# Chunk attention: half-row sums shared between GpSimd and VectorE, and an order planned with longer VectorE durations

## The chip, the cores and the metric

The kernel runs on one core of a Trainium2 chip. The metric is device time in microseconds (us), lower is better. A profiled execution gives the trace from which every row below comes; its times are those of that one execution.

## The reference, cut to what matters

Three layers run one after the other on 8 sequences of 576 tokens. Only the first one and the routing of the second are touched.

```python
# 1. attention inside chunks of 64 tokens, 8 heads of 64
scores = scale * np.matmul(q_c, k_c.transpose(0, 1, 2, 4, 3))
scores = scores - np.max(scores, axis=-1, keepdims=True)
attn = np.exp(scores)
attn = attn / (np.sum(attn, axis=-1, keepdims=True) + 1e-09)
out = np.matmul(attn, v_c)
# 2. one of 8 experts per token; a token takes a fresh choice or the choice of the token before it
h = np.maximum(x[b, s] @ w1[e], 0.0)
out[b, s] = p[e] * (h @ w2[e])
# 3. four causal attention experts, the two best mixed per token
```

## The kernel before, in words

**Stages.** `chunk_attention` (line 166) works through 36 tiles of 128 tokens. The expert layer follows, then the causal mix. In the trace the first stage with all routing lasts until about 234 us, the experts until 660 us, the mix to the end.

**A tile.** q and k are loaded in pairs of tiles, turned by TensorE (L277) and copied out by ScalarE (L292, L295). TensorE makes the scores (L315). VectorE takes the row maximum (L326, 512 columns on 128 partitions, 64 per head) and subtracts it (L330). ScalarE takes the exponential (L334). Then VectorE sums each row of exponentials (L335), adds 1e-9 (L336) and takes the reciprocal (L337). Meanwhile TensorE turns the exponentials (L261 `at`), they are copied out (L344), multiplied by v (L354), and VectorE scales the product by the reciprocal (L363, tile `xs`). GpSimd issues the store of `xs` to the scratch tensor `x_d` (L368). TensorE turns `xs` too (L261 `xs`), and L390 and L405 make the gate logits, which VectorE collects (L408, tile `L`).

**Routing.** After every 9 tiles `route_group` (line 482) runs a chain of small steps that goes back and forth between VectorE and TensorE: from L504 through the turn L523, the scans L534, the turns L541 and L554, the choice L564 to L573, the counts L580 and L584, to the bit split L601 to L605 and the table `lo` (L619). After the third of four groups `route_early` (line 658) sums slot numbers for the first expert by 27 matmuls (L670, the early slot sum) and VectorE turns them into row indices (L652 to L656, `gfirst`). With these GpSimd fetches rows of `x_d` (L703). Two blocks of 256 tokens of the first expert are computed while the last tiles and the last routing group still run: `early_pair` (line 675) turns the fetched rows (L715), multiplies by w1 (96 matmuls of 256 columns a block, written L1620 to L1622, "up" here) and, for the first block, by w2 (48 matmuls of 512 columns, "down"). `route_all` (line 786) takes all four groups: VectorE builds the one-hot slot table (L817) and its products (L823; half on GpSimd), TensorE sums it by 36 matmuls (L832, the full slot sum), VectorE makes `gidx` (L655), GpSimd fetches the next block's rows (L839), and the first instruction of the expert stage on TensorE turns them (L954).

**Order.** None of this is issued in the order of the code. Every step is put into a `Plan` with an engine, a cost in us, a due key and the steps and buffers it waits for; `emit` picks, step by step, the earliest start by these costs, and the order that comes out is fixed for each engine. Engines then run in that order and wait by semaphores. So a cost in the code moves instructions but does not change how long one takes.

Of the kernel before, what the change touches and what calls it, by code (L numbers as in the profile page):

```python
# [14 lines left out]
OP = mybir.AluOpType  # L15
AX = mybir.AxisListType
# [97 lines left out]
class Model:  # L114
# [51 lines left out]
    def chunk_attention(self):  # L166
# [5 lines left out]
        with ExitStack() as ctx:  # L172
# [11 lines left out]
            R = {name: Ring(n) for name, n in (("q", 2), ("k", 2), ("tq", 2), ("one", 4),  # L184
                                               ("qT", 2), ("st", 5), ("at", 4), ("aT", 2), ("xs", 3), ("xT", 2), ("lp", 2))}

# [117 lines left out]
            def token_tile(t):  # L304
# [29 lines left out]
                x = plan.add("ACT", act(512), lambda: A.activation(box["at"], box["at"], AF.Exp, scale=0.125), t, [d2])  # L334
                d3 = plan.add("DVE", dve(512), lambda: V.tensor_reduce(box["st"][:, 1], box["at"], axis=AX.X, op=OP.add), t + 0.5, [x])  # L335
                d4 = plan.add("DVE", 0.08, lambda: V.tensor_scalar(box["st"][:, 1], box["st"][:, 1], 1e-9, None, op0=OP.add), t + 1.5, [d3])  # L336
                d5 = plan.add("DVE", 0.12, lambda: V.reciprocal(box["st"][:, 2], box["st"][:, 1]), t + 1.5, [d4])  # L337

# [7 lines left out]
                tp.users.append(y)  # L346
                sat.users += [ft, d3]
                px = R["px"].slot()
# [133 lines left out]
    def route_group(self, g):  # L482
# [18 lines left out]
        def bank():  # L501
            return self.psum(RING, [128, 512])
        small, mid = 0.08, 0.145
        step("DVE", mid, lambda: V.tensor_reduce(r["mx"], Lg, axis=AX.X, op=OP.max))  # L504
# [13 lines left out]
        box = {}  # L518
# [13 lines left out]
        def scans():  # L532
            box["kp"], box["sv"] = T([GT, 128], "kp"), T([GT, 128], "sv")
            V.tensor_tensor_scan(box["kp"], box["pr"][:, 1], r["zeros"], 1.0, op0=OP.mult, op1=OP.add)  # L534
            V.tensor_tensor_scan(box["sv"], box["pr"][:, 1], box["rise"], 0.0, op0=OP.mult, op1=OP.add)
        q.users.append(step("DVE", 0.4, scans))
        q = R[RING].slot()
# [24 lines left out]
        def chosen():  # L562
            box["ef"] = T([GT, 128], "rise")
            V.scalar_tensor_tensor(box["ef"], box["kp"], box["cin"], box["sv"], op0=OP.mult, op1=OP.add)  # L564
        step("DVE", 0.26, chosen)
        q = R[RING].slot()
# [31 lines left out]
        def bits():  # L598
# [6 lines left out]
            V.tensor_copy(r["hi"][:, ts], si[:, 2])  # L605
        ranked = step("DVE", 0.6, bits)
        self.placed = getattr(self, "placed", [])
        if g < self.NG - 1:
            K = self.K

            def early():
                x = r["erows"][:, ts, 0]
                V.tensor_tensor(x, r["hi"][:, ts, None].to_broadcast([128, GT, K]),
                                r["slotn"][:, None, :K].to_broadcast([128, GT, K]), op=OP.is_equal)
                V.tensor_tensor(x, x, oh[:, 0, :, None].to_broadcast([128, GT, K]), op=OP.mult)
                V.tensor_tensor(r["erows"][:, ts, 1], x, r["tnum"][:, ts, None].to_broadcast([128, GT, K]), op=OP.mult)
                V.tensor_scalar(x, x, r["part"], None, op0=OP.mult)
            self.placed.append(step("DVE", 0.45, early))
        low = step("DVE", 1.27, lambda: V.tensor_tensor(r["lo"][:, ts], r["lane"][:, None, :].to_broadcast([128, GT, 128]),  # L619
                                                        box["sf"][:, :, None].to_broadcast([128, GT, 128]), op=OP.is_equal))  # L620
# [37 lines left out]
    def route_early(self):  # L658
# [8 lines left out]
        def gather():  # L667
            x = box["pi"] = self.psum(self.RING, [128, 512])[:, :2 * K]
            for t in range(n):
                nc.tensor.matmul(x, r["lo"][:, t], r["erows"][:, t].rearrange("p a s -> p (a s)"), start=t == 0, stop=t == n - 1)  # L670
        step("PE", 0.064 * n, gather, takes=[q])
        self.early_at = step("DVE", 0.5, lambda: self.places(box["pi"].rearrange("p (a s) -> p a s", a=2), K, self.gfirst, self.sfirst))
        q.users.append(self.early_at)
# [1018 lines left out]
```

## Time and profile before

| | |
|---|---|
| median of 3 runs | 1083.32 us (1082.28 to 1086.37) |
| the profiled execution | 1081.1 us |
| its span | 1079.3 us |
| TensorE busy | 1027.4 us, 95% |
| VectorE busy | 689.1 us, 64% |
| ScalarE busy | 596.9 us, 55% |
| GpSimd busy | 337.1 us, 31% |

TensorE's matmuls overlap each other, so its busy time is time in which at least one of them runs. Its idle time, and its granted clock, are what the other engines and the order cost. VectorE's share is an average: it is far higher in the first stage than later.

### The profile page before, as it was taken

The page shows a single profiled execution, that of the slowest core. Times are in us where ns is not written, and L with a number is a line of the kernel's source. Part 1 is how long each engine was busy: PE and PEld are TensorE (multiplying, and loading weights), DVE is VectorE, ACT ScalarE, POOL GpSimd, SP SyncE. Part 2 cuts the span into 40 slices and gives each one's busy share as a digit, 9 for nine tenths or more (in the row PEclk, how much of TensorE's full clock was granted, in tenths as well). Part 3 has the DMA queues.
Part 4 walks back from the last instruction along what each step waited for, and adds up shares of the span by engine and source line. Part 5 has one row for each costly group of instructions (what it writes and reads, how often), then busy time and mean ns, then how long its engine had stood idle before and what let it go on. Part 6 is the DMA issues. An engine that isn't in the chain of part 4 may idle for free. (4 is left out here: it accounts for less than half of the span.)

```text
span 1079.3 us, 23454 instructions
## 1 busy us (share of the span) xinstructions
PE 1027.4 (95%) x7767; PEld 917.6 (85%) x7767; DVE 689.1 (64%) x1770; ACT 596.9 (55%) x1379; POOL 337.1 (31%) x586
## 2 busy tenths in 40 slices
PE   7999897999999998999999999999999999999996
PEld 5877776899899887998898996988999999999985
DVE  6678888564552245435623421597888888898884
ACT  5988986223441135315512310577777777777774
POOL 3111354232242232322422312143334243343431
PEclk9999998999999999999999999999999999999998
DMA  9999982145543154334622311434252432525231
GB/s 222 232 253 242 267 247 87 59 144 177 181 140 128 42 163 134 131 128 141 216 98 99 116 49 54 125 84 100 66 137 70 127 86 93 122 67 127 65 84 50
DMA packets 136476, 138.98 MB, mean 129 GB/s; under 512 B 54724, under 2 KB 108024, under 8 KB 134264
## 3 DMA queue, kind: packets, MB, share of 16 engines
q1 hardware_dynamic: 116584, 99.66, 34.3%
q0 software_dynamic: 12592, 35.18, 9.8%
q10 hardware_dynamic: 7136, 2.11, 0.8%
q8 instruction: 84, 1.38, 0.5%
q14 instruction: 80, 0.66, 0.2%
HBM read 89.70 MB, written 29.64 MB: 111 GB/s over the span
## 5 line engine op out<-in xcount | busy, mean ns | idle before, releaser
L1620 PE MATMUL ph<-xh,w 128*128 128x256 f32 x512 | 142.4, 278 | 4.4 <-ACTq L1062 2.6
L1622 PE MATMUL ph<-xh,w 128*128 128x256 f32 x512 | 142.3, 278 | 0.3 <-DVE w L877 0.3
L1621 PE MATMUL ph<-xl,w 128*128 128x256 f32 x512 | 142.0, 277 | 0.0
L970 ACT ACTIVATE hh<-ph 128x512 fp32r<-128x512 f32 x64 | 37.9, 598 | 182.7 <-PE ph L1622 182.6
L1042 POOL DMA_INDIRECT y_d<-ys,sidx x39 | 39.5, 1012 | 284.2 <-DVE ys L1037 213.4
L1453 POOL TENSOR_SCALAR a<-a,st,g_out 128x128 f32<-128x128 f32 (+3 forms) x128 | 79.5, 622 | 85.4 <-DVE st L1448 58.6
L1032 PE MATMUL py<-w,hh 128*128 128x512 f32 x280 | 104.5, 398 | 0.3 <-issue 0.3
L971 DVE SCALAR_TENSOR_TENSOR hl<-ph,hh 128x512 fp32r<-128x512 f32 x64 | 43.4, 688 | 93.8 <-ACT hh L970 65.3
L1620 PEld LDWEIGHTS ph<-xh,w 128*128 128x128 f32 x512 | 96.1, 188 | 6.5 <-ACTq L1062 3.8
L1622 PEld LDWEIGHTS ph<-xh,w 128*128 128x128 f32 x512 | 96.5, 189 | 0.5 <-DVE w L877 0.5
L1621 PEld LDWEIGHTS ph<-xl,w 128*128 128x128 f32 x512 | 96.3, 188 | 0.5
L1037 DVE TENSOR_SCALAR ys<-py,pg 128x512 f32<-128x512 f32 x37 | 27.7, 749 | 104.5 <-PE py L1034 82.3
L1437 ACT ACTIVATE a<-sc,st 128x256 f32<-128x256 f32 (+4 forms) x160 | 83.0, 521 | 20.4 <-DVE st L1429 14.9
L1032 PE MATMUL py<-w,hl 128*128 128x512 f32 x232 | 90.9, 392 | 0.0
L1429 DVE TENSOR_REDUCE st<-sc 128x1 f32<-128x256 f32 (+4 forms) x160 | 75.8, 482 | 4.4
L877 DVE TENSOR_TENSOR w<-raw,w 128x512 fp32r<-128x512 f32 (+1 forms) x84 | 67.1, 865 | 16.6 <-ACT w L876 12.2
L1252 ACT ACTIVATE at<-tp 128x128 fp32r<-128x128 f32 (+2 forms) x144 | 65.1, 455 | 22.4 <-PE tp L1470 20.4
L1253 DVE TENSOR_TENSOR at<-tp,at 128x128 fp32r<-128x128 f32 (+2 forms) x144 | 72.3, 505 | 7.5 <-ACT at L1252 6.1
L1470 PE MATMUL tp<-ident,a 128*128 128x128 f32 (+1 forms) x400 | 69.6, 276 | 7.2 <-DVE at L1253 3.5
L1034 PE MATMUL py<-w,hh 128*128 128x512 f32 x280 | 69.8, 391 | 0.0
L1418 PE MATMUL sc<-kd,qs 128*128 128x128 f32 (+3 forms) x256 | 62.8, 338 | 4.2 <-ACT a L1437 3.4
L876 ACT ACTIVATE w<-raw 128x512 fp32r<-128x512 f32 (+1 forms) x84 | 57.3, 761 | 16.9 <-DMA wst<-in_moe_wq_dram 6.0
(335 smaller groups left out, 2881.6 us busy)
## 6 DMA issues: line engine op xcount, KB each, us to landing
raw<-in_moe_w_dram SPq DMA_DIRECT2D x32, 1024.0 KB, 6.6
kd<-kb SPq DMA_DIRECT2D x64, 160.0 KB, 3.0
vb<-in_v_dram SPq DMA_DIRECT2D x144, 64.0 KB, 4.4
x_d<-xs POOLq DMA_DIRECT2D x36, 256.0 KB, 4.0
yt<-y_d SPq DMA_DIRECT2D x32, 256.0 KB, 2.7
kd<-kb SPq DMA_DIRECT2D x64, 128.0 KB, 2.4
out_dram<-zs SPq DMA_DIRECT2D x32, 256.0 KB, 2.0
q<-in_q_dram SPq DMA_DIRECT2D x11, 512.0 KB, 5.5
```

The lines of the kernel that those rows point to most:

```text
L877: (engine or self.nc.vector).tensor_tensor(lo, src, as_f32(hi), op=OP.subtract)
L1032: nc.tensor.matmul(py[m], h[:, j, ms], W2[0][:, j], start=h is hh and j == 0, stop=False)
L1034: nc.tensor.matmul(py[m], hh[:, j, ms], W2[1][:, j], start=False, stop=j == JF - 1)
L1252: h = plan.add("ACT", act(n), lambda: A.activation(hi, src(), AF.Copy), key, dep)
L1253: l = plan.add("DVE", dve(n), lambda: V.tensor_tensor(lo, src(), as_f32(hi), op=OP.subtract), key, [h])
L1429: V.tensor_reduce(st[:, i:i + 1], box["sc"][i][:, :k1 - k0], axis=AX.X, op=OP.max, negate=True)
L1437: A.activation(a[:, k0:k1], box["sc"][i][:, :k1 - k0], AF.Exp, bias=st[:, 0:1], accum_out=st[:, 3 + i:4 + i])
L1453: (P if ext <= PX else V).tensor_scalar(a[:, :ext], a[:, :ext], st[:, 6:7], gate, op0=OP.mult, op1=OP.mult)
L1470: nc.tensor.transpose(ta[:c1 - c0, kc - k0], box["a"][:, c0:c1], self.ident)
L1620: self.nc.tensor.matmul(out, ah, bh, start=first and i == 0, stop=False)
L1621: self.nc.tensor.matmul(out, ah, bl, start=False, stop=False)
L1622: self.nc.tensor.matmul(out, al, bh, start=False, stop=last and i == n - 1)
```

## The change

The sum of each row of 64 exponentials is split. GpSimd adds the two halves of each row (two inputs of 256 columns, new tile `half`, one buffer), VectorE sums the 32 that are left (256 columns instead of 512), GpSimd adds the 1e-9, and VectorE takes the reciprocal. Apart from this only costs in the plan change, nearly all of them upward, and the `lp` ring has one buffer instead of two. In the changed kernel the lines after L335 stand 7 lower: the half sum is L341, 1e-9 is L343, the reciprocal L344, `xs` L370, the last gate turn L412, the turn of the routing L530, the row turn L722, the table `lo` L626, the full slot sum L839, the expert stage's first turn L961.

```diff
-               d3 = plan.add("DVE", dve(512), lambda: V.tensor_reduce(box["st"][:, 1], box["at"], axis=AX.X, op=OP.add), t + 0.5, [x])
-               d4 = plan.add("DVE", 0.08, lambda: V.tensor_scalar(box["st"][:, 1], box["st"][:, 1], 1e-9, None, op0=OP.add), t + 1.5, [d3])
-               d5 = plan.add("DVE", 0.12, lambda: V.reciprocal(box["st"][:, 2], box["st"][:, 1]), t + 1.5, [d4])
+               hslot = R["half"].slot()
+
+               def halve():
+                   box["half"] = sb("half", [128, H, C // 2])
+                   P.tensor_tensor(box["half"], box["at"][:, :, :C // 2], box["at"][:, :, C // 2:], op=OP.add)
+               d2 = plan.add("POOL", 0.55, halve, t + 0.5, [x], [hslot])
+               d3 = plan.add("DVE", dve(256), lambda: V.tensor_reduce(box["st"][:, 1], box["half"], axis=AX.X, op=OP.add), t + 0.5, [d2])
+               hslot.users.append(d3)
+               d4 = plan.add("POOL", 0.22, lambda: P.tensor_scalar(box["st"][:, 1], box["st"][:, 1], 1e-9, None, op0=OP.add), t + 1.5, [d3])
+               d5 = plan.add("DVE", 0.2, lambda: V.reciprocal(box["st"][:, 2], box["st"][:, 1]), t + 1.5, [d4])
...
-       small, mid = 0.08, 0.145
+       small, mid = 0.14, 0.17
...
-       q.users.append(step("DVE", 0.4, scans))
+       q.users.append(step("DVE", 0.75, scans))
...
-       ranked = step("DVE", 0.6, bits)
+       ranked = step("DVE", 0.85, bits)
...
-           self.placed.append(step("DVE", 0.45, early))
+           self.placed.append(step("DVE", 1.2, early))
...
-       step("PE", 0.064 * n, gather, takes=[q])
+       step("PE", 0.03 * n, gather, takes=[q])
```

What the new costs move is seen in the orders. The first place is VectorE (DVE) behind the second routing group, at the copy of its probabilities (`kp`) and after. `st` holds a tile's maxima, sums and reciprocals. Before:

```order
L326 TENSOR_REDUCE st<-one 128x8
L336 TENSOR_SCALAR st<-st 128x8
L326 TENSOR_REDUCE st<-one 128x8
L330 TENSOR_TENSOR at<-one,st 128x512
L363 TENSOR_TENSOR xs<-one,st 128x512
L337 RECIPROCAL st<-st 128x8
L330 TENSOR_TENSOR at<-one,st 128x512
L335 TENSOR_REDUCE st<-at 128x8
L363 TENSOR_TENSOR xs<-one,st 128x512
L344 COPY aT<-one 128x512
```

The same place in the changed kernel:

```order
L344 RECIPROCAL st<-st 128x8
L651 COPY kp<-one 9x128
L370 TENSOR_TENSOR xs<-one,st 128x512
L341 TENSOR_REDUCE st<-half 128x8
L326 TENSOR_REDUCE st<-one 128x8
L330 TENSOR_TENSOR at<-one,st 128x512
L344 RECIPROCAL st<-st 128x8
L370 TENSOR_TENSOR xs<-one,st 128x512
L326 TENSOR_REDUCE st<-one 128x8
L330 TENSOR_TENSOR at<-one,st 128x512
```

The sums read `half` instead of `at`, and the 1e-9 step is gone from VectorE.

The second place is TensorE (PE) between the last gate turn (`lp`) and the first turn of the last routing group (`keep`). `tq<-q,w` is an "up" matmul of the first early block, `tq<-w,raw` a "down" matmul. Before, 36 up matmuls stand between the two, the first and the last of them here:

```order
L405 MATMUL one<-ident,lp 128x128 x2
L1620 MATMUL tq<-q,w_0_83 128x256
...
L1622 MATMUL tq<-q,w_1_84 128x256
L523 MATMUL one<-ident,keep 9x128
L524 MATMUL one<-ident,w 9x128
```

In the changed kernel:

```order
L412 MATMUL one<-ident,lp 128x128 x2
L1627 MATMUL tq<-q,w_0_83 128x256
...
L1629 MATMUL tq<-q,w_1_84 128x256
L722 MATMUL one<-ident,raw_81 128x128 x8
L1627 MATMUL tq<-w_0_85,raw_3006 128x512
...
L530 MATMUL one<-ident,keep 9x128
L531 MATMUL one<-ident,w 9x128
```

Of the 96 up matmuls of the first block, 84 stand ahead of the last gate turn and 12 behind it (48 and 48 before), and 8 turns and 18 down matmuls have come ahead of `keep`.

The third place is TensorE at the full slot sum (`one<-raw,lo`), up to the first turn of the expert stage (`pxt`). Before, 48 up matmuls of the second early block stand between them:

```order
L832 MATMUL one<-raw_81,lo 128x108
L1620 MATMUL tq<-q,w_0_83 128x256
L1621 MATMUL tq<-k,w_0_83 128x256
...
L1622 MATMUL tq<-q,w_1_84 128x256
L954 MATMUL pxt<-ident,raw_81 128x128 x8
```

In the changed kernel:

```order
L1628 MATMUL tq<-k,w_0_83 128x256
L1629 MATMUL tq<-q,w_1_84 128x256
L839 LDWEIGHTS lo
...
L839 MATMUL one<-raw_81,lo 128x108
L961 MATMUL pxt<-ident,raw_81 128x128 x8
```

All 96 up matmuls of the second block stand ahead of the slot sum, and the expert stage's turns follow it directly.

## Rows read from the trace of the kernel before

**Rows 1.** Windows: busy us and instructions of each engine, TensorE's clock, DMA share, GB/s.

```profile
20.00:160.00 140.00, 131.13 (x1562) 107.28 (x1560) 113.14 (x294) 124.35 (x220) 34.89 (x52) 1.00 1.00 249
125.00:145.00 20.00, 16.26 (x191) 13.21 (x189) 19.86 (x52) 16.30 (x28) 7.75 (x8) 1.00 0.89 223
234.00:450.00 216.00, 211.76 (x1356) 190.87 (x1357) 94.58 (x130) 73.40 (x119) 63.10 (x62) 1.00 0.45 147
```

**Rows 2.** Timeline of TensorE: start us, us, instruction, idle before and its releaser.

```profile
90.56 1.09 PE L277 MATMUL tq<-ident,k 128*128 128x128 f32 x8 [1.87 <-ACT kb L295]
...
127.55 1.09 PE L277 MATMUL tq<-ident,q 128*128 128x128 f32 x8 [1.38 <-ACT qT L292]
...
143.87 0.66 PE L261 MATMUL one<-ident,xs 128*128 128x128 f32 x4 [1.09 <-DVE xs L363]
```

**Rows 3.** Groups by form: busy us, mean ns of one, idle before.

```profile
L335 DVE TENSOR_REDUCE st<-at 128x8 f32<-128x512 f32 x36 | 24.3, 678 | 8.9 <-ACT at L334 8.8
L336 DVE TENSOR_SCALAR st<-st 128x8 f32<-128x8 f32 x36 | 8.0, 224 | 0.2
L1429 DVE TENSOR_REDUCE st<-sc 128x1 f32<-128x256 f32 x48 | 20.2, 421 | 1.1
L900 POOL TENSOR_TENSOR w<-raw,w 128x512 fp32r<-128x512 f32 x8 | 10.2, 1281 | 10.1 <-ACT w L899 10.0
L1653 POOL TENSOR_TENSOR g_eq<-g_eq,lower 128x80 f32<-128x80 f32 x4 | 1.4, 358 | 0.6 <-DVE g_eq L1639 0.4
L1446 POOL TENSOR_SCALAR st<-st 128x1 f32<-128x1 f32 x144 | 31.3, 217 | 104.6 <-ACT a L1437 97.8 <-DVE sc L1427 1.1
```

**Rows 4.** Timeline of GpSimd and of VectorE at two of GpSimd's subtractions.

```profile
129.31 2.36 POOL L900 TENSOR_TENSOR w<-raw,w 128x1024 fp32r<-128x1024 f32 x1 [1.45 <-ACT w L899]
...
140.24 2.37 POOL L900 TENSOR_TENSOR w<-raw,w 128x1024 fp32r<-128x1024 f32 x1 [0.80 <-ACT w L899]
...
129.47 2.26 DVE L615 TENSOR_TENSOR erows<-erows,oh 128x36 bf16<-128x36 bf16 x1
...
140.45 2.17 DVE L336 TENSOR_SCALAR st<-st 128x8 f32<-128x8 f32 x1
```

**Rows 5.** Early slot sum and row fetch: TensorE, VectorE, GpSimd, DMA issues (us to landing).

```profile
173.29 0.59 PE L670 MATMUL one<-erows,lo 128*128 128x8 bf16 x18 [0.80 <-ACT aT L344]
178.16 0.40 PE L670 MATMUL one<-erows,lo 128*128 128x8 bf16 x9 [4.28 <-DVE lo L619]
...
186.81 1.12 PE L715 MATMUL one<-ident,raw 128*128 128x128 f32 x8
...
176.76 1.35 DVE L619 TENSOR_TENSOR lo<-lane,sf 128x1152 bf16<-128x1152 bf16 x1
...
181.81 1.03 POOL L703 DMA_INDIRECT raw<-x_d,gfirst  x1 [5.88 <-issue]
...
raw<-x_d,gfirst POOLq DMA_INDIRECT x4, 3.8
```

**Rows 6.** Window behind that wait, columns as in rows 1.

```profile
178.00:182.00 4.00, 3.84 (x39) 3.51 (x41) 3.48 (x14) 0.63 (x1) 0.19 (x1) 0.52 0.02 4
```

**Rows 7.** TensorE from the last gate turn to the expert stage, then VectorE.

```profile
199.49 0.38 PE L405 MATMUL one<-ident,lp 128*128 128x128 f32 x2
...
204.01 0.27 PE L523 MATMUL one<-ident,keep 128*9 128x128 f32 x1
...
211.74 0.21 PE L580 MATMUL one<-oh,ones 128*128 128x72 bf16 x1
...
224.67 1.90 PE L832 MATMUL one<-raw,lo 128*128 128x108 bf16 x36
232.22 0.65 PE L954 MATMUL pxt<-ident,raw 128*128 128x128 f32 x4
233.10 0.75 PE L954 MATMUL pxt<-ident,raw 128*128 128x128 f32 x4 [0.24 <-DMA raw<-x_d,gidx]
...
221.57 2.41 DVE L823 TENSOR_TENSOR raw<-raw,tnum 128x972 bf16<-128x972 bf16 x1
```

More of the change, by code (lines that the diff above doesn't have):

```diff
@@ L184, in chunk_attention @@
             R = {name: Ring(n) for name, n in (("q", 2), ("k", 2), ("tq", 2), ("one", 4),
-                                               ("qT", 2), ("st", 5), ("at", 4), ("aT", 2), ("xs", 3), ("xT", 2), ("lp", 2))}
+                                               ("qT", 2), ("st", 5), ("half", 1), ("at", 4), ("aT", 2), ("xs", 3), ("xT", 2), ("lp", 1))}
             R["tp"] = R["sc"] = R["px"] = R["pl"] = R["one"]
@@ L346, in token_tile @@
                 tp.users.append(y)
-                sat.users += [ft, d3]
+                sat.users += [ft, d2]
                 px = R["px"].slot()
@@ L564, in chosen @@
             V.scalar_tensor_tensor(box["ef"], box["kp"], box["cin"], box["sv"], op0=OP.mult, op1=OP.add)
-        step("DVE", 0.26, chosen)
+        step("DVE", 0.33, chosen)
         q = R[RING].slot()
@@ L617, in early @@
                 V.tensor_scalar(x, x, r["part"], None, op0=OP.mult)
-            self.placed.append(step("DVE", 0.45, early))
-        low = step("DVE", 1.27, lambda: V.tensor_tensor(r["lo"][:, ts], r["lane"][:, None, :].to_broadcast([128, GT, 128]),
+            self.placed.append(step("DVE", 1.2, early))
+        low = step("DVE", 1.4, lambda: V.tensor_tensor(r["lo"][:, ts], r["lane"][:, None, :].to_broadcast([128, GT, 128]),
                                                         box["sf"][:, :, None].to_broadcast([128, GT, 128]), op=OP.is_equal))
@@ L670, in gather @@
                 nc.tensor.matmul(x, r["lo"][:, t], r["erows"][:, t].rearrange("p a s -> p (a s)"), start=t == 0, stop=t == n - 1)
-        step("PE", 0.064 * n, gather, takes=[q])
-        self.early_at = step("DVE", 0.5, lambda: self.places(box["pi"].rearrange("p (a s) -> p a s", a=2), K, self.gfirst, self.sfirst))
+        step("PE", 0.03 * n, gather, takes=[q])
+        self.early_at = step("DVE", 0.9, lambda: self.places(box["pi"].rearrange("p (a s) -> p a s", a=2), K, self.gfirst, self.sfirst))
         q.users.append(self.early_at)
```

## The prediction

> **What bounds the kernel now.** I read the windows by stage first. From 20 to 160 us, in the chunk attention, TensorE is busy 131.1 of 140 us, ScalarE 124.4, VectorE 113.1, GpSimd 34.9, and the DMA share is 1.00 [rows 1]. TensorE is the bound there, with 8.9 us of idle; VectorE is not, on average. Behind 234 us TensorE is busy 211.8 of 216 us [rows 1], so what happens earlier moves the end about one for one.
>
> Then I looked for the 8.9 us in TensorE's timeline. The largest pieces lie where a routing group's small steps compete with the tiles on VectorE: 1.87 us at 90.6, 1.38 us at 127.6, 1.09 us at 143.9, the last of them until a tile `xs`, the others until a copy of ScalarE [rows 2]. From 125 to 145 us VectorE is busy 19.9 of 20 us and TensorE idle 3.7 [rows 1]. In this stretch VectorE is the bound.
>
> Last, the places where routing hands over to matmul work. TensorE waits 0.80 and 4.28 us for the table `lo` in the early slot sum [rows 5], and after it runs at about half the full clock until 182, the lower of its two levels (1.2 of 2.4 GHz) [rows 6]. At the hand-over to the experts it waits only 0.24 us for the fetched rows [rows 7]: the chain from the last gate turn (ends about 199.7) through routing and fetch to the second turn at 233.1 takes 33.4 us, and just that much matmul work lies beside it.
>
> **The change, part by part.**
>
> *Sum and 1e-9.* VectorE loses 678 ns for the full sum and 224 ns for the 1e-9, and gains a sum of 256 columns, 421 ns by the nearest row, a sum of 128x256 [rows 3]. That is 0.48 us a tile, 17.3 us in 36 tiles. On TensorE's path it counts only where VectorE is saturated. In the 20 us from 125 to 145 pass about 4.5 tiles (the 36 tiles take some 160 us), so 2.2 us; there also lies the one 1e-9 step that took 2.17 us instead of about 0.16 [rows 4], which leaves VectorE: 2.0 us more. Together 4.2, which covers the 3.7 us of idle. Of the other 5.1 us I give a third, 1.7, because they end on ScalarE more often than on VectorE [rows 2], and ScalarE is busy 89% itself. Gain 5.4 us; the bounds are 0 and 8.9.
>
> *GpSimd's new work.* The half addition has two inputs of 256 columns. Between 358 ns (80 columns) and 1281 ns (512) [rows 3] a line gives 0.73 us; with 217 ns for the 1e-9, 0.95 us a tile, 34 us in all, on an engine that is busy 35 of 140 us. I cost it at nothing. What hides it is that the product waits meanwhile for the turn of the exponentials, their copy and the multiplication by v. That cover goes where a half addition stands behind one of the 12 subtractions of expert weights (1.28 us for 512 columns, 2.4 for 1024): the half sum waits on VectorE, and behind it in VectorE's order wait the next tile's maximum and shift. Bounds: 0, and 12 times half of about 1.65 us, 10 us.
>
> GpSimd and VectorE also stop each other: of two VectorE steps of about 0.2 us, one took 2.26 and one 2.17 us, and both end with a subtraction on GpSimd [rows 4]. The Trainium skill (SBUF — State Buffer, "Who interferes with whom") says that a VectorE instruction with two SBUF inputs, or one in a 2-port mode, is blocked for the whole of a GpSimd instruction that reads SBUF. That speaks against the change, since it adds 36 such instructions, and for it, since the 1e-9 step leaves VectorE. The two long steps of rows 4 are of these kinds: one has two SBUF inputs, the other goes from SBUF to SBUF. By that rule maximum, shift and scaling, which read PSUM, are not touched, and the routing steps are exposed: a half addition runs 0.73 of 4.4 us, some 20 exposed steps a group would meet 3 or 4 and wait about 0.37 us each, 1.3 us a group; by that the sum would be 1 to 3 us higher.
>
> *The early slot sum.* TensorE waits 5.1 us there. Between the counts and the end of `lo` VectorE's order has three tile operations (about 0.6 us each, as they follow one another closer than the 0.68 of one); the changed order has one, so 1.2 us less, and one turn of `xs` (0.5 us) has been put ahead of the sum. The wait becomes about 3.4 us, gain 1.7. Bounds: gain 0 to 5.1. I leave the slow clock behind it as it is.
>
> *The row turn.* The first fetch is issued 3.7 us after the end of `lo` (178.1 to 181.8) and lands 3.8 us later [rows 5]: 7.5 us. Before, 8.2 us of tile work lay between the end of the sum (178.6) and the turns (186.8) [rows 5]. In the changed order only a gate step, one multiplication by v, the gate turn, two score steps and two turns lie there, 4.6 us, and VectorE still puts about as much (a copy, a half sum, a maximum, a shift) between `lo` and the indices. A new wait of up to 2.5 us; I take 2.0, as the clock is low there and stretches the cover. Bounds: 0 and 4.
>
> *The hand-over.* This is the largest term. 36 more up matmuls stand ahead of the last gate turn. 36 of them took from 199.6, when the gate turn made way, to 204.0 [rows 7], 0.12 us each: the last logits come 4.3 us later in the same work. That alone costs nothing, but the chain behind them has 4.3 us less to lie beside, and it is longer itself. Until `keep` there are now 12 up, 8 turns and 18 down. Just these lay between `keep` and the counts before, 7.7 us [rows 7], with some 0.5 us of small routing turns; so 7.2 us instead of 4.4: +2.8. From `keep` to the counts there are 30 down. 18 took 7.2 less 12 up (1.45) and 8 turns (1.1 [rows 5]), 4.6, so 0.25 each: with the small turns 8.0 instead of 7.7 us: +0.3. From the counts to the slot products' end 12.2 us (211.7 to 224.0); the changed order has four full-width operations of 0.65 in it instead of two, +1.3. Then the slot sum, which stood 0.7 us behind other matmuls, starts at once: -0.6. From there to the second turn 8.4 us as before. Sum +3.8; with 4.3 it is **8.1 us**. As a check, by cover: in front of the slot sum TensorE has about 26 us of work and VectorE needs about 28.3, so 2.3 idle; behind it, 8.4 less the sum (1.9) and the first turns (0.65), 5.9 us: 8.2, against 0.24 before [rows 7]. Bounds: 4 (if the chain does not lengthen) and 11 (if GpSimd's fetches hold the last tile's half addition, which now queues behind them).
>
> *The clock.* After 5.1 us of waiting the clock was about half up to 182 [rows 5, 6]: the 3.8 us from 178.2 did half as much, so 1.9 us were lost. A second such gap at the hand-over costs as much again: 1.9. Bounds 0 and 3.
>
> *The `lp` ring.* One buffer instead of two: the next pair's gate sums come some 8 us later, the turn frees it within 1 us. Nothing.
>
> Sum: -5.4 - 1.7 + 2.0 + 8.1 + 1.9 = **+4.9 us**. The profiled execution took 1081.1 us, of them 1079.3 span; it becomes 1086.0. The median of the runs shown, 1083.3, is 2.2 above it, so the forecast is 1088.
>
> **Rivals.**
>
> *The stage becomes tight and the early waits go.* If the longer costs place the routing steps well, all 8.9 us go, and the wait of 5.1 with its slow clock, 1.9. With no wait at the row turn the sum is -15.9 + 8.1 = -7.8, or 1075.5 by the median. For it: VectorE is full exactly where TensorE idles. Against: two of the three waits in rows 2 end on a copy of ScalarE, and ScalarE has no work less. It decides if the idle time before 160 us falls under 2 us.
>
> *GpSimd holds the half sums.* The other bound of GpSimd's work: 10 us on VectorE, of which the stage has slack for half. +5 on the forecast, 1093. For it: GpSimd runs in order and already has steps of 2.4 us; only one buffer of `half` exists. Against: GpSimd is 75% idle in the stage. It decides where half sums on VectorE sit waiting for GpSimd by more than 5 us in all.
>
> *The stage is held by the transfers.* The DMA share is 1.00 over 140 us [rows 1]. If loads land later as the stage speeds up, the 5.4 us do not come: 1093. Against: none of TensorE's large waits ends on a load [rows 2].
>
> *The hand-over keeps its cover.* If the last tile's chain ends early and the routing steps run ahead of their planned place, only 4 us are lost, no clock: about 1083. Against: TensorE runs in a fixed order, and `keep` stands behind the down matmuls whatever VectorE does.
>
> **How the numbers follow.** Chances: the forecast 0.58, tight stage 0.15, GpSimd 0.13, transfers 0.06, cover kept 0.08. The forecast's own range is +0.5 to +9 (1084 to 1092). What a measurement of this kernel can tell from no change is about 0.5%, 5.4 us; the forecast lies just below it, and I put 0.24 of its 0.58 above. Slower: 0.24 + 0.12 + 0.05 = 0.41. Faster: most of the tight stage, 0.12. Same: 0.47. The range leaves a tenth at each side: 1078 to 1097.
>
> **What would show it.** In the changed profile VectorE's 125 to 145 us should no longer be full and TensorE's idle from 20 to 160 should be near 3.5 us. The half sum should take about 0.42 us and the half addition about 0.73. TensorE should wait about 3 us at the early slot sum, about 2 at the row turn, and about 8 us in all from the last gate turn to the expert stage's second turn, with the lower clock level right after. The forecast is wrong if that last gap is under 3 us, or if the idle before 160 us does not fall.

## The result, and the profile after

The changed kernel takes 1096.46 us (median of 4 runs, 1094.28 to 1100.37), the kernel before in the same session 1084.84 (1082.28 to 1086.46): a ratio of 1.0115, 95% interval 1.0088 to 1.0143. It is slower, by 11.6 us where 4.9 were forecast. Its profiled span is 1094.3 us (before: 1079.3), the mean granted clock 0.984 (0.991).

Windows of the changed kernel, columns as in [rows 1]:

```profile
20.00:160.00 140.00, 132.18 (x1510) 107.19 (x1512) 95.41 (x254) 120.92 (x212) 60.46 (x104) 0.96 0.93 238
125.00:145.00 20.00, 16.74 (x172) 14.08 (x170) 14.21 (x45) 14.92 (x25) 10.61 (x13) 0.83 0.83 209
245.00:250.00 5.00, 4.20 (x13) 3.18 (x14) 1.38 (x2) 1.19 (x2) 1.56 (x2) 0.50 0.72 179
...
120.00:125.00 5.00, 5.00 (x50) 3.95 (x48) 2.60 (x8) 2.92 (x5) 0.84 (x2) 0.66 1.04 260
130.00:135.00 5.00, 3.06 (x15) 2.66 (x16) 3.59 (x14) 4.14 (x7) 2.60 (x1) 0.61 0.95 236
135.00:140.00 5.00, 5.00 (x46) 3.91 (x45) 2.00 (x5) 2.09 (x3) 2.04 (x6) 0.71 0.80 201
185.00:192.00 7.00, 6.92 (x68) 4.84 (x66) 5.31 (x16) 1.96 (x4) 4.16 (x6) 0.70 0.23 61
```

VectorE lost what it was to lose: 95.4 us busy instead of 113.1 up to 160 us, 14.2 instead of 19.9 from 125 to 145. TensorE did not gain: its busy time from 125 to 145 is 16.7 us against 16.3, with a granted clock of 0.83 instead of 1.00, so that less is done in it (172 matmul records instead of 191). From 20 to 160 us TensorE's idle time fell only from 8.9 to 7.8 us, where 3.5 was foretold, and its mean granted clock fell from 1.00 to 0.96: the low stretches are 120 to 125 us (0.66) and 130 to 140 (0.61 and 0.71).

The new instructions cost what was estimated. Groups by form, columns as in [rows 3]:

```profile
L339 POOL TENSOR_TENSOR half<-at 128x256 f32<-128x256 f32 x36 | 26.5, 736 | 44.1 <-ACT at L334 43.4
...
L341 DVE TENSOR_REDUCE st<-half 128x8 f32<-128x256 f32 x36 | 14.7, 408 | 5.6 <-POOL half L339 5.6
...
L343 POOL TENSOR_SCALAR st<-st 128x8 f32<-128x8 f32 x36 | 8.2, 228 | 20.9 <-DVE st L341 19.6
```

The half addition takes 0.74 us (0.73 estimated), the half sum 0.41 (0.42), the 1e-9 0.23 (0.22). TensorE's timeline where it now waits longest in the tiles, columns as in [rows 2]:

```profile
127.64 0.60 PE L261 MATMUL one<-ident,at 128*128 128x128 f32 x4
128.08 0.60 PE L277 MATMUL tq<-ident,k 128*128 128x128 f32 x4
130.78 1.70 PE L277 MATMUL tq<-ident,q 128*128 128x128 f32 x8 [2.10 <-ACT qT L292]
133.63 1.97 PE L277 MATMUL tq<-ident,k 128*128 128x128 f32 x8 [1.16 <-ACT kb L295]
135.40 0.42 PE L646 MATMUL one<-ident,sm 128*9 128x128 f32 x1
135.75 1.98 PE L361 MATMUL one<-vb,aT 128*64 128x128 f32 x16
```

Eight q turns and eight k turns stand in a row and wait for ScalarE's copies. The multiplication by v (L361) of a tile whose exponentials were turned at 127.6 stands behind them, at 135.8; it takes 1.98 us where it takes 1.09 at the full clock. The early slot sum (TensorE, then VectorE), columns as in [rows 5]:

```profile
183.22 1.11 PE L261 MATMUL one<-ident,xs 128*128 128x128 f32 x4 [4.02 <-DVE xs L370]
184.12 0.91 PE L677 MATMUL one<-erows,lo 128*128 128x8 bf16 x27
...
182.48 0.68 DVE L370 TENSOR_TENSOR xs<-one,st 128x512 f32<-128x512 f32 x1
183.08 1.35 DVE L626 TENSOR_TENSOR lo<-lane,sf 128x1152 bf16<-128x1152 bf16 x1
```

The 4.28 us in front of `lo` [rows 5] are a wait of 4.02 now, one instruction earlier: the turn of `xs` that was put ahead of the sum waits for a scaling that VectorE does only behind the routing steps, just before `lo`. From the row turns to the expert stage on TensorE, answering to [rows 7]:

```profile
192.15 0.72 PE L722 MATMUL one<-ident,raw 128*128 128x128 f32 x4
...
194.50 0.72 PE L722 MATMUL one<-ident,raw 128*128 128x128 f32 x4
...
210.49 0.38 PE L412 MATMUL one<-ident,lp 128*128 128x128 f32 x2
...
217.22 0.27 PE L530 MATMUL one<-ident,keep 128*9 128x128 f32 x1
...
238.41 2.00 PE L839 MATMUL one<-raw,lo 128*128 128x108 bf16 x36 [1.15 <-ACT raw L831]
245.57 1.13 PE L961 MATMUL pxt<-ident,raw 128*128 128x128 f32 x4 [5.15 <-DMA raw<-x_d,gidx]
246.93 1.13 PE L961 MATMUL pxt<-ident,raw 128*128 128x128 f32 x4 [0.23 <-DMA raw<-x_d,gidx]
```

The row turns do not wait. At the hand-over TensorE waits 1.15 + 5.15 + 0.23 = 6.5 us, against 0.24 [rows 7], and runs at 0.50 of the clock behind it (245 to 250 above).

**Where it was lost.** Start-up differs from run to run (the `xs` of the 5th tile comes at 38.3 to 42.3 us), so I measure from the scaling (`xs`) of the 5th tile to the second turn of the expert stage, cut at the `xs` of the 29th tile, the end of the early slot sum, the start of the last gate turn, and the end of the full slot sum. The first line is in us, the others are differences to it, each from one profile. The names are those of the experiments below. Where a kernel has the order before, its pieces repeat within 0.2 us (E7, E8 and E13 in the stretches that they leave alone). In the tiles of the changed order they do not: E12 has the changed kernel's instructions and order up to about 195 us, and its tiles show +1.0 against +4.0 (see E12). So differences of up to 3 us in the first column mean nothing for kernels with that order, and a total that rests on them is no finer than the medians; the sum differs from the difference of the medians by up to 2.9 us (E11). The last column is the ratio of medians to the kernel before, with its 95% interval.

| kernel | tiles 5 to 29 | to end of early slot sum | to last gate turn | to end of full slot sum | to second turn | sum | ratio |
|---|---|---|---|---|---|---|---|
| before, us | 117.4 | 22.9 | 20.9 | 27.1 | 6.5 | 194.9 | 1 |
| changed | +4.0 | +2.1 | +4.5 | +2.8 | 0.0 | +13.5 | 1.0115 (1.0088, 1.0143) |
| E1 old costs, halves | +1.8 | +1.9 | +4.7 | +1.7 | -0.1 | +9.9 | 1.0091 (1.0061, 1.0121) |
| E2 new costs alone | +3.5 | +1.7 | -4.3 | +1.3 | +2.6 | +4.7 | 1.0019 (0.9998, 1.0039) |
| E3 old order, new instructions | +5.0 | +1.6 | +4.6 | 0.0 | -0.1 | +11.1 | 1.0070 (1.0042, 1.0099) |
| E4 new order, old instructions | +2.7 | +3.0 | +5.0 | +2.9 | -0.2 | +13.3 | 1.0124 (1.0083, 1.0165) |
| E5 old order, VectorE relieved | -2.2 | -0.3 | +0.3 | 0.0 | -0.1 | -2.3 | 0.9969 (0.9950, 0.9988) |
| E6 new order, VectorE relieved | +2.1 | +1.6 | +4.6 | +2.9 | -0.2 | +11.0 | 1.0093 (1.0061, 1.0124) |
| E7 new order, old tail | +3.2 | 0.0 | -0.2 | 0.0 | -0.1 | +3.0 | 1.0056 (1.0037, 1.0076) |
| E8 old order, new tail | +0.1 | +3.0 | +4.4 | +2.9 | 0.0 | +10.4 | 1.0086 (1.0059, 1.0113) |
| E9 changed, three moves | +1.7 | +3.6 | +4.5 | +2.8 | -0.1 | +12.5 | 1.0087 (1.0072, 1.0102) |
| E10 old order, late half sum | +1.0 | +1.1 | +2.1 | -0.1 | -0.2 | +4.0 | 1.0031 (1.0016, 1.0046) |
| E11 before without 1e-9 | +0.2 | 0.0 | +1.0 | 0.0 | -0.2 | +1.1 | 0.9984 (0.9975, 0.9993) |
| E12 changed, old tail from the row turn | +1.0 | +2.2 | +7.0 | 0.0 | -0.2 | +10.0 | 1.0101 (1.0085, 1.0117) |
| E13 before, gate turn later | 0.0 | 0.0 | +4.4 | -2.4 | -0.2 | +1.9 | 1.0008 (0.9995, 1.0020) |
| E14 old order, unread halves | +1.0 | +1.4 | 0.0 | 0.0 | -0.2 | +2.3 | 1.0005 (0.9986, 1.0023) |

Behind the second turn the profiles differ by -1.3 to +4.1 us, and the changed kernel's +1.2 there means nothing by itself. The six kernels with a late hand-over (changed, E1, E4, E6, E8, E9) have +2.5 there on average, the ten others +0.5.

### The profile page after: what moved, and what is told of

It reads as the page before. It is cut to its first block, busy times and chain, and to the rows that moved or that the text cites. A ratio compares the mean times of both kernels' runs of the same rounds, so it can differ in the third digit from the quotient of the medians.

```text
span 1094.3 us, 23574 instructions
## 1 busy us (share of the span) xinstructions
PE 1035.2 (95%) x7767; PEld 921.5 (84%) x7767; DVE 675.0 (62%) x1734; ACT 597.1 (55%) x1379; POOL 373.0 (34%) x658
## 5 line engine op out<-in xcount | busy, mean ns | idle before, releaser
L1259 ACT ACTIVATE at<-tp 128x128 fp32r<-128x128 f32 (+2 forms) x144 | 65.1, 454 | 22.9 <-PE tp L1477 20.9
L884 DVE TENSOR_TENSOR w<-raw,w 128x512 fp32r<-128x512 f32 (+1 forms) x84 | 67.0, 866 | 16.3 <-ACT w L883 13.3
L1453 POOL TENSOR_SCALAR st<-st 128x1 f32<-128x1 f32 x144 | 31.0, 216 | 104.7 <-ACT a L1444 97.9
L883 ACT ACTIVATE w<-raw 128x512 fp32r<-128x512 f32 (+1 forms) x84 | 57.3, 761 | 16.7 <-PE py L1039 6.0
```

The source lines that it names most:

```text
L884: (engine or self.nc.vector).tensor_tensor(lo, src, as_f32(hi), op=OP.subtract)
L1259: h = plan.add("ACT", act(n), lambda: A.activation(hi, src(), AF.Copy), key, dep)
```

## The experiments

**E1 and E2: the costs and the halves apart.** E1 is the changed kernel with the eight routing costs put back, E2 the kernel before with the eight new ones.

```diff
 E1, in the changed kernel (8 such lines)
-       q.users.append(step("DVE", 0.75, scans))
+       q.users.append(step("DVE", 0.4, scans))
 E2, in the kernel before (the same lines the other way)
-       q.users.append(step("DVE", 0.4, scans))
+       q.users.append(step("DVE", 0.75, scans))
```

> The changed kernel with the old costs of the routing steps; the halved sums stay. Theory A: two places cost the 12 us. The loss of 5 us around the second routing group (115 to 137 us) comes from the new routing costs, the late end of routing at the hand-over from the halved sums on GpSimd. Then the loss around 115 to 137 us is gone and the hand-over keeps about 6.5 us of TensorE idle: about 1090 us, 5 over before. Rival B: the halved sums bring both, and the costs nothing: about 1096. Rival C: the costs bring both: about 1084, hand-over wait under 1 us.

> The kernel before with the new costs of the routing steps alone; sum and 1e-9 stay on VectorE as before. Theory A: the loss around the second routing group appears (TensorE 4 to 5 us behind from there on), the hand-over to the experts has under 1 us of idle: about 1090 us. Rival B (halved sums bring both): 1080 to 1085, no loss anywhere. Rival C (costs bring both): 1096 with over 5 us of idle at the hand-over.

E1 took 1095.06 us (rival B), E2 1087.42 against 1084.64. So the halved sums, with what they do to the plan, bring most of the loss; the costs alone cost 2.8 us by the medians, which is not clear of nothing (at most 0.39% by the interval). E2's pieces show that this is no agreement with the order before: it loses 5.2 us up to the early slot sum, gets 4.3 of them back before the last gate turn and loses 3.9 behind it.

**E3 and E4: the order and the instructions apart.** E3 keeps the order before: where VectorE's sum stood, GpSimd's half addition and VectorE's half sum are issued one behind the other, and the 1e-9 goes to GpSimd. E4 keeps the changed order and has VectorE do full sum and 1e-9.

```diff
 E3, in the kernel before
+               def sums():
+                   half = sb("half", [128, H, C // 2])
+                   P.tensor_tensor(half, box["at"][:, :, :C // 2], box["at"][:, :, C // 2:], op=OP.add)
+                   V.tensor_reduce(box["st"][:, 1], half, axis=AX.X, op=OP.add)
-               d3 = plan.add("DVE", dve(512), lambda: V.tensor_reduce(box["st"][:, 1], box["at"], ...
+               d3 = plan.add("DVE", dve(512), sums, t + 0.5, [x])
 E4, in the changed kernel
-                   P.tensor_tensor(box["half"], box["at"][:, :, :C // 2], box["at"][:, :, C // 2:], op=OP.add)
+                   pass
-               d3 = ... V.tensor_reduce(box["st"][:, 1], box["half"], ...
+               d3 = ... V.tensor_reduce(box["st"][:, 1], box["at"], ...
```

> The order of the kernel before, unchanged on TensorE, ScalarE and VectorE, with the new instructions in it: half addition and 1e-9 on GpSimd (the half addition stands in GpSimd's order where VectorE's sum was), half-row sum on VectorE. If the order is the cause of the loss (theory A), this keeps the early part level, frees 0.48 us a tile on VectorE and has no idle at the hand-over: 1078 to 1085 us. If GpSimd's work itself is the cause (half sums waiting for GpSimd on VectorE, more than 5 us in all), it loses what the change loses: 1090 or more.

> The order of the changed kernel, with the old instructions in it: no half addition, VectorE sums full rows where it sums half rows in the change and adds 1e-9 itself. If the order is the cause, it loses as much as the change or more, since VectorE has 17 us more to do: 1096 to 1102 us, over 5 us of idle at the hand-over. If GpSimd's work is the cause, it is near before: 1084 to 1089.

E3 took 1093.61 us, E4 1098.64. In E3 the theory that the order is the only cause failed, in E4 it held. Each alone costs about as much as the change: the order, without any of the work that it was planned for, 14.0 us; the new instructions in the order before, 9.0. In E3 VectorE waits for GpSimd (waits of VectorE, 20 to 165 us: us in total, times, longest):

```profile
DVE st L341 <- POOL half L340: 30.8, 25, 2.6
DVE st L345 <- POOL st L344: 1.7, 5, 0.4
```

The same view of the changed kernel:

```profile
DVE st L341 <- POOL half L339: 3.6, 6, 0.8
DVE st L344 <- POOL st L343: 2.4, 3, 1.6
```

The changed order does hide most of that wait: 6.0 us are left of 32.5.

**E5 and E6: what VectorE's relief is worth.** The half sum is taken straight from the exponentials, so half of each row is left out of the sum, and the 1e-9 is left out; GpSimd has nothing new.

```diff
 E5, in the kernel before; E6 does the same in the changed kernel, with an empty half addition
-               ... V.tensor_reduce(box["st"][:, 1], box["at"], axis=AX.X, op=OP.add)
+               ... V.tensor_reduce(box["st"][:, 1], box["at"][:, :, :C // 2], axis=AX.X, op=OP.add)
-               d4 = plan.add("DVE", 0.08, lambda: V.tensor_scalar(box["st"][:, 1], box["st"][:, 1], 1e-9, ...
+               d4 = plan.add("DVE", 0.08, lambda: None, t + 1.5, [d3])
```

> The order before the change; VectorE sums only the first 32 of each row of 64 exponentials (the other half is left out of the sum) and the 1e-9 step is left out; GpSimd does nothing new. VectorE loses the same 17 us as by the change. Theory V (the forecast's term: VectorE's relief is worth 5.4 us before 160 us): 1079. Theory S (TensorE's waits in this order end on ScalarE and on the order, the relief is worth little): 1083 to 1085. Against 1093.6 for the same order with GpSimd's half additions, the difference is what waiting for GpSimd costs there: 14 us by V, 9 to 10 by S.

> The changed order; as above, half of each sum and the 1e-9 left out, nothing new on GpSimd. If GpSimd's work is hidden in the changed order (as the forecast said, costed at nothing): 1095 to 1097, like the change. If GpSimd in the changed order holds VectorE (the rival with half sums waiting): 1090 or less.

E5 took 1082.23 us (2.4 less than before, between the two theories; 1.3 to 5.4 by the interval of the ratio), E6 1095.04, as expected if GpSimd's work is hidden. By pieces the relief brings 2.3 us in the old order; in the new one it is 3.6 by the medians (E4 to E6, in two sessions). Windows of E5, columns as in [rows 1]:

```profile
20.00:160.00 140.00, 131.63 (x1566) 108.00 (x1568) 102.19 (x267) 125.35 (x221) 35.11 (x52) 1.00 0.98 250
125.00:145.00 20.00, 17.89 (x218) 14.51 (x219) 17.83 (x51) 18.32 (x32) 8.15 (x9) 1.00 0.96 243
```

From 125 to 145 us VectorE is no longer full (17.8 of 20), and TensorE still idles 2.1 of its 3.7 us: of these 1.4 end on a copy of ScalarE (L292) and 0.5 on VectorE. From E6 to the changed kernel GpSimd's work adds 1.4 us by the medians, within the spread; the 13.5 - 11.0 = 2.5 us by pieces lie in tiles that do not repeat within 3 us.

**E7 and E8: the two halves of the order.** Old instructions, and the two orders joined behind the `xs` of the 27th tile (about 150 us): E7 has the changed one first, E8 last.

```diff
-           plan.emit(window=80, slack=0)
+           follow(plan, ORDER)
+def follow(plan, order):
+    for i in order:
+        plan.steps[i].fn()
```

> The old instructions; the changed order up to the scaling of the 27th tile (about 150 us), the order before the change from there on. The changed order as a whole with the old instructions cost 14 us. Theory T (two separate losses, about 5 us at 117 to 137 and about 9 from the early slot sum to the hand-over): 1089 to 1091, the hand-over waits under 1 us. Rival (what is lost early is what makes the hand-over late): 1095 or more.

> The old instructions; the order before the change up to the scaling of the 27th tile, the changed order from there on. Theory T: 1092 to 1095, with 5 to 7 us of waits at the hand-over. Rival (the early loss makes the hand-over late, the tail by itself costs nothing): 1084 to 1087.

E7 took 1090.11 us, E8 1094.52, both in theory T's ranges. The two losses are separate and add up: 5.5 and 9.9 us by the medians, 15.4 in all, where the whole order (E4) has 14.0; by pieces 3.0 and 10.4, where E4 has 13.3. The hand-over of E7, then of E8:

```profile
235.41 0.65 PE L954 MATMUL pxt<-ident,raw 128*128 128x128 f32 x4
236.22 0.75 PE L954 MATMUL pxt<-ident,raw 128*128 128x128 f32 x4 [0.17 <-DMA raw<-x_d,gidx]
```

```profile
236.03 2.05 PE L832 MATMUL one<-raw,lo 128*128 128x108 bf16 x36 [1.17 <-POOL raw L823]
243.17 1.10 PE L954 MATMUL pxt<-ident,raw 128*128 128x128 f32 x4 [5.09 <-DMA raw<-x_d,gidx]
244.59 1.13 PE L954 MATMUL pxt<-ident,raw 128*128 128x128 f32 x4 [0.32 <-DMA raw<-x_d,gidx]
```

What is lost in the tiles does not make the hand-over late, and the hand-over is late without it.

**E9: three moves in the tiles.** In the changed kernel VectorE's shift (L330) of tile 24 goes ahead of the second group's routing steps, and on TensorE the multiplication by v (L361) of tile 22 and the turn L646 go ahead of the q and k turns shown above. The order list is followed as in E7.

```diff
-  L412 L261 L277(k) L277(q x8) L277(k x8) L646 L361
+  L412 L261 L277(k) L361 L646 L277(q x8) L277(k x8)
```

> The changed kernel (1096.5) with three instructions moved at 127 to 136 us and nothing else: on VectorE the shift of tile 24 ahead of the routing chain of the second group instead of behind it; on TensorE the multiplication by v of tile 22 and the turn of the routing's probabilities ahead of the eight q turns and eight k turns that wait there for ScalarE's copies. Theory O (the order of this place is what loses 4 to 6 us): 1091 to 1094, no wait over 1.5 us at these turns, the clock up. Rival (ScalarE's copies bound this place whatever TensorE does ahead of them): 1096 to 1097.

E9 took 1095.64 us: about 1 us better by the median, which does not separate the theories. The timeline of TensorE there:

```profile
130.49 1.09 PE L361 MATMUL one<-vb,aT 128*64 128x128 f32 x16 [0.24 <-ACT aT L351]
131.95 0.27 PE L646 MATMUL one<-ident,sm 128*9 128x128 f32 x1 [0.37 <-DVE si L608]
132.40 1.09 PE L277 MATMUL tq<-ident,q 128*128 128x128 f32 x8 [0.17 <-ACT qT L292]
135.24 1.09 PE L277 MATMUL tq<-ident,k 128*128 128x128 f32 x8 [1.75 <-ACT kb L295]
```

The wait of 2.10 is gone and the matmuls are at their full speed, while the k turns still wait for ScalarE. The tiles' loss is 1.7 us instead of 4.0, and the piece behind them 3.6 instead of 2.1. But E12, which has none of these moves, lost only 1.0 in its tiles. So the moves take the wait and the low clock out of this place, while what the place is worth is not shown, and it does not reach the end. The clock was low in E9 too, at 0.72 from 120 to 125 us.

**E10 and E11: looking for a better kernel.** E10 keeps the order before, with the half addition where the sum stood, the half sum where the 1e-9 stood (the one buffer of `half` moves six steps by a place), and no 1e-9: the row's maximum gives exp(0) = 1, so a sum is at least 1, and 1e-9 does not change it in float32. E11 is the kernel before without the 1e-9.

```diff
 E11
-               d4 = plan.add("DVE", 0.08, lambda: V.tensor_scalar(box["st"][:, 1], box["st"][:, 1], 1e-9, ...
+               d4 = plan.add("DVE", 0.08, lambda: None, t + 1.5, [d3])
```

> The order before the change. GpSimd's half addition stands where VectorE's full sum stood, the half sum of VectorE where the 1e-9 step stood, and the 1e-9 step is left out on both engines (the maximum of a row gives exp(0) = 1, so a sum is at least 1 and 1e-9 does not change it in float32). VectorE loses as much as in the run with half the sum left out (1082.2), and has the time between the two places for GpSimd's 0.73 us. If GpSimd's work then lies beside the tile's chain: 1081 to 1083, faster than both kernels. If GpSimd's order holds the half sums in spite of it: 1086 to 1092.

> The kernel before the change without the 1e-9 step of VectorE (36 steps of 0.16 to 0.22 us, one of 2.17), everything else as it was. Where VectorE is saturated (125 to 145 us) it has 4 to 5 of them and the long one: 1082 to 1083. If that place is not bound by VectorE: 1084 to 1085.

E10 took 1088.16 us, E11 1083.02 against 1084.79. E10's half sums still wait, as its second case had it:

```profile
DVE st L341 <- POOL half L339: 6.1, 6, 1.7
```

E11 is the only version here that computes everything and beats both kernels, by 1.8 us (0.07 to 0.25%). Its one profile does not show where (its pieces are not shorter).

**E12 and E13: the hand-over alone.** E12 is the changed kernel up to the first copy of fetched rows (about 195 us), with the order before from there on. E13 is the kernel before with one instruction of TensorE moved.

```diff
 E13, rows of TensorE's order
-  L405 (last gate turn)   36 up matmuls   L523 (keep)
+  36 up matmuls   L405 (last gate turn)   L523 (keep)
```

> The changed instructions; the changed order up to the first copy of the fetched rows of the first early block (about 195 us), the order before the change from there on, so that 48 instead of 84 of the first block's up matmuls stand ahead of the last gate turn and 48 of the second block's behind the full slot sum. Theory T (the hand-over alone loses the 8.1 and the clock 1.2 to 1.9 of the forecast): 1087 to 1089. Rival (these matmuls only change places, the loss lies ahead of the first early block): 1094 to 1096.

> The kernel before the change with one instruction moved: the last gate turn on TensorE stands behind all 36 up matmuls that stood between it and the first turn of the last routing group, as in the changed order; the routing that follows from it starts by as much later. Theory C (the hand-over is held by the chain from the last gate turn to the fetched rows, and what stands ahead of it is lost from its cover): 4.3 us are lost, as a wait at the first turn of the last routing group, 1088 to 1090. Rival (the chain catches up, the cover is kept): 1084 to 1086.

E12 took 1095.44 us, which is not distinguished from the changed kernel (ratios 1.0101 and 1.0115). Its hand-over has no wait left, and two new ones stand earlier:

```profile
194.83 0.72 PE L722 MATMUL one<-ident,raw 128*128 128x128 f32 x4 [2.49 <-issue]
...
200.09 1.09 PE L261 MATMUL one<-ident,xs 128*128 128x128 f32 x4 [2.39 <-DVE xs L370]
...
243.73 1.38 PE L961 MATMUL pxt<-ident,raw 128*128 128x128 f32 x8
```

The up matmuls that cover the hand-over are missing at the last tiles instead: the piece to the last gate turn grows from +4.5 to +7.0, and most of the gain goes back. The expectation that this alone returns 8 us was wrong. Whether these two waits come from the order of the last tiles or from the joint of the two orders was not separated.

E12 also shows how far one profile of the tiles can be trusted. Up to the `xs` of the 19th tile it keeps step with the changed kernel within 0.2 us; by that of the 24th it is 3.0 us ahead, with the same instructions in the same order. Its windows there:

```profile
120.00:125.00 5.00, 5.00 (x67) 3.83 (x67) 3.40 (x10) 3.88 (x7) 1.64 (x3) 1.00 1.02 293
130.00:135.00 5.00, 3.24 (x21) 2.59 (x21) 2.86 (x7) 3.15 (x5) 3.71 (x3) 0.69 1.14 267
135.00:140.00 5.00, 5.00 (x70) 4.32 (x68) 2.94 (x6) 3.60 (x7) 2.95 (x3) 0.97 0.90 247
```

Before 120 us TensorE waited 1.11 us for ScalarE's copy there and kept its full clock; in the changed kernel it waited 1.58 us and went down to 0.66.

E13 took 1085.36 us, near the rival:

```profile
205.68 0.38 PE L405 MATMUL one<-ident,lp 128*128 128x128 f32 x2
207.74 0.28 PE L523 MATMUL one<-ident,keep 128*9 128x128 f32 x1 [1.68 <-DVE keep L515]
```

VectorE's steps from the gate turn to `keep` need 2.06 us; before, 4.5 us of matmuls lay beside them [rows 7]. So 2.5 of the 4.4 us by which the gate turn is later come back at once, and 1.9 are lost by pieces (0.6 by the medians, not clear of nothing).

**E14: GpSimd's work without anyone waiting for it.** E5 with the half additions put back at E3's places; nobody reads their result. As in E5, half of each row and the 1e-9 are left out of the sum.

```diff
 E14, in E5
+                   P.tensor_tensor(half, box["at"][:, :, :C // 2], box["at"][:, :, C // 2:], op=OP.add)
                    V.tensor_reduce(box["st"][:, 1], box["at"][:, :, :C // 2], axis=AX.X, op=OP.add)
```

> The order before the change; VectorE sums only half of each row straight from the exponentials, the 1e-9 is left out (1082.2 without GpSimd's work), and GpSimd adds the halves at the same places as in the run of the old order with the new instructions (1093.6), but nobody reads or waits for its result. Theory W (what GpSimd's work costs is the wait of VectorE for it): 1081 to 1083.5. Theory P (GpSimd's additions slow VectorE or stand ahead of GpSimd's other work, stores and weight subtractions): 1085 or more.

E14 took 1085.18 us, just inside theory P: 3.0 more than E5 by the medians (the two were timed in different sessions, against 1084.79 and 1084.63), 4.6 by pieces. With the wait and the 1e-9 on GpSimd (E3) it is another 8.4 by the medians, 8.8 by pieces. A part of the price is seen in E14's timeline (VectorE and GpSimd, as in [rows 4]):

```profile
176.16 0.56 POOL L372 DMA_DIRECT2D x_d<-xs  x1
176.27 2.45 DVE L608 CAST sf<-si 128x9 f32<-128x9 int32 x1
176.74 0.73 POOL L337 TENSOR_TENSOR half<-at 128x256 f32<-128x256 f32 x1
...
177.42 1.27 POOL L904 TENSOR_TENSOR w<-raw,w 128x512 fp32r<-128x512 f32 x1
```

A cast of 9 columns, 0.17 us elsewhere, ends only behind a half addition and the subtraction that follows it. It lies in the chain to the early slot sum, and that piece is 1.7 us longer than E5's. The other half of theory P, that GpSimd's own stores and subtractions come later, was not run apart.

## Why the prediction was right or wrong

The direction was right and the time lies in the range; the size was not. The step that failed is the first term of the sum, **the steady gain of 5.4 us, with GpSimd's new work "at nothing"** and no term for the order of the tiles, and behind it the early slot sum.

*Sum and 1e-9, -5.4.* In place of the gain the tiles became longer, by 4.0 us in the changed kernel's profile and by 1.0 in E12's. Three things stand in this place. VectorE's relief is worth 2.4 us by the medians of E5, and the forecast 5.4 is the very end of its interval: VectorE was full from 125 to 145 us, but only about half of TensorE's idle time there was due to it, and the third of the rest that was added was too much. GpSimd's work was set at the end of its bounds (0 to 10); in the changed order it costs 1.4 us by the medians, which is not clear of nothing. And the order of the tiles had no term at all: it alone costs 5.5 us by the medians (E7; 4.0 to 8.2 by the interval). The prediction followed the order at the early slot sum and at the hand-over, and took it as neutral where the tiles run. There it put q turns ahead of other matmuls, where they wait for ScalarE's copies (1.58 us at 119.3, 2.10 at 130.8, and 1.16 for the k turns), and the clock is low behind these waits. An estimate from the three low windows: (1 - 0.66) x 5.00 + (1 - 0.61) x 3.06 + (1 - 0.71) x 5.00 = 4.3 us of TensorE's time, about what its tiles became longer. Why the clock stayed up in one of these places in E12 is open.

*The rule on shared ports.* The sum was to be 1 to 3 us higher by it. The Trainium skill (SBUF — State Buffer, "Who interferes with whom") says that a VectorE instruction with two SBUF inputs contends with a GpSimd instruction that reads SBUF, and one in a 2-port mode with GpSimd, and that whoever issues first holds the shared ports for the whole instruction. The cast of 2.45 us in E14, an operation from SBUF to SBUF, fits that; no run here shows its mode. The size was not borne out in the changed kernel: the small VectorE steps that took over 0.3 us more than usual, up to 195 us, add up to 9.1 us of excess before (7 steps) and 6.4 in the changed kernel (8 steps). In the order before, the half additions raise them from 7.4 (E5) to 9.4 us (E14), of the 3.0 by which E14 is slower.

*The early slot sum, -1.7.* The wait fell only from 5.1 to 4.4 us (4.02, and 0.35 at the routing turn L646 ahead of it), and the piece up to the end of the sum grew by 2.1. The turn that was counted as cover waits itself for VectorE. VectorE has fewer tile operations among the routing steps, as foretold, but three of these steps took 0.77, 1.23 and 1.19 us beside GpSimd's work, where two took 1.14 and 1.15 before. GpSimd's new work is not needed for the longer piece: E4, E6 and E8, which lack it, have +3.0, +1.6 and +3.0.

*The row turn, +2.0.* No wait. The seven steps that were counted as 4.6 us of cover took 7.0 us (185.1 to 192.1), as the clock was at 0.70 there; L361 took 1.98 us. That the low clock stretches the cover was said, but with 0.5 us, where it was 2.4.

*The hand-over, +8.1.* By pieces +4.5 + 2.8 = 7.3, by waits 6.5 against the 8.2 of the check by cover: right within 2 us. The old instructions with the new tail (E8) show the same waits, so it is the order's doing. But the working by chain had a slack that it did not see: a later gate turn alone costs 1.9 us by pieces (E13), not 4.3. And in E12, with the up matmuls back in their places, the last gate turn is later still, so where they stand may not be the whole cause.

*The clock, +1.9.* The granted clock is 0.50 behind the hand-over, as foretold. Behind the second turn the six kernels with a late hand-over lose 2.0 us more on average than the others, near the 1.9, though the single profiles scatter by more than that. Not foretold were the low stretches in the tiles, which by the estimate above cost about as much as the whole loss there.

All terms behind the steady gain came to -1.7 + 2.0 + 8.1 + 1.9 = 10.3 in the forecast; the order's tail measured by itself (E8) costs 10.4 by pieces, 9.3 by the ratio. That the sums agree is partly luck, as the slot sum and the row turn were both off. With the 5.4 forecast as a gain and 4.0 lost, this profile is off by 9.4 in the tiles; the medians are off by 11.6 - 4.9 = 6.7.

*The rivals.* The tight stage did not come: the idle time before 160 us is 7.8 us, not under 2. "GpSimd holds the half sums" came true in part: VectorE waited 5.6 us for half additions in all, just over the point named; but the same order without GpSimd's work (E6) is nearly as slow, so it did not decide. The transfers did not hold the stage (DMA share 0.93 instead of 1.00, and TensorE waited only 0.2 us for a load). The hand-over did not keep its cover; the sum given for that rival, with 4 for 8.1 and no clock, comes to -1.1 and so to 1082, not 1083.

## What to carry to other kernels

A change that passes through a planner is two changes, and each can be run without the other: the new order with the old instructions, the old order with the new ones. Here each alone cost about 1%, while the instructions' own saving, 17 us of VectorE, was worth 2.4 us. Relief of an engine counts only for the waits that end on it, and giving work to an idle in-order engine can cost both the wait for it and the neighbours that it stops. And a piece read from one profile carries the clock of that execution: the same order gave +4.0 and +1.0 here.

## What the runs showed of the hardware

One VectorE instruction can be held through two GpSimd instructions in a row: 2.45 us in E14 across an addition of 0.73 and a subtraction of 1.27. In the changed kernel a comparison (L513) took 2.30 us, from 162.48 to 164.78, across the ends of two subtractions and the DMA issue between them. TensorE's k turns and multiplication by v took 1.97 and 1.98 us instead of 1.09 after waits of 2.10 and 1.16 us, the granted clock being 0.61 from 130 to 135 us and 0.71 from 135 to 140. One order of the same instructions kept the full clock from 120 to 125 us in one execution (E12) and fell to 0.66 in another (the changed kernel).
